# Loading the first chunk's q and k in rows of 1 KB by halves of the heads, and masking the third tile on VectorE

## The chip, the core and the metric

The kernel runs on one core of a Trainium2 chip. The metric is device time in microseconds (us); lower is better. Before the change it is 223.19 us, the median of 3 runs (222.91 to 223.42). TensorE multiplies matrices, VectorE (DVE) and ScalarE (ACT) work on tiles, GpSimd (POOL) does small work and issues DMAs, and SyncE (SP) issues DMAs; ACT can issue them too.

## What is computed

Windowed attention with sinks over 4 batches, 8 heads, 768 tokens and a head size of 64, then a normalised MLP with a residual. Inputs and output are float32.

```python
scores = scale * np.matmul(q, k.transpose(0, 1, 3, 2))
keep = is_sink | in_window          # 4 sinks, window of 128 tokens, causal
scores = np.where(keep, scores, -1000000000.0)
a = softmax(scores)
x = matmul(a, v), heads side by side  # [4, 768, 512]
xn = (x - mu) / np.sqrt(var + 1e-06) * g_ln
out = x + np.maximum(xn @ w_ch1, 0.0) @ w_ch2   # w_ch1 512 x 2048, w_ch2 2048 x 512
```

## The kernel before

The 3072 tokens are 24 tiles of 128; two tiles are a chunk, three chunks a batch. For each tile the kernel gets q and k with the head dimension on the partitions (`kT`, `qT`: four head pairs of 128 rows), computes transposed scores against its own and the preceding tile's keys (L681, L726), takes the exponential on ScalarE (`ex`, L685 and L740) and multiplies by v (`av`, L763 and L768). VectorE divides by the row sum (`rec` L781, `x` L783), takes the statistics (`st` L787, L789) and subtracts the mean (`xc` L791). `xc` is transposed (L804), scaled into `xnt` (L815), and goes through the MLP: `ph` (L830 by tile for the first two chunks, L837 by chunk after), relu (`h`, L847 on ScalarE, L849 on VectorE), `pc` (L866), the residual (L874) and the store (L878).

Nothing is issued in program order. Every operation is entered with `P.op` as a record of the engines that may run it, their times, a priority, and its dependences. `Plan.run` then walks a model of the engines and DMA queues, and what it finds is written out as each engine's fixed order. Constants such as `HW_F` (the model of the first loads: time a DMA keeps the queue, its start, its end) change nothing on the chip but the order. An engine runs its list strictly in that order and waits at the first instruction that is not ready. A ring is a set of buffers taken in turn; `pair` is two slots of two PSUM banks each, for scores and values, `one` single banks.

The first chunk (tiles 0 and 1 of batch 0) is loaded apart from the others. `chunk(0)` issues four DMAs of 256 KB in float32, k on SP and q on ACT (L563): for each tile, partitions 0 to 63 hold k and 64 to 127 hold q, two neighbouring tokens to a partition, which makes rows of 2 x 64 x 4 = 512 B in `natf`. ScalarE and VectorE each cast four heads to bf16 (`natc`, L570); eight matmuls with the identity turn the tile (L580), and their outputs are interleaved in PSUM, so that the two tokens of a partition come to stand next to each other; ScalarE and VectorE evict them into `kT` and `qT` (L547). Tiles 2 and 3 come by GpSimd's DMAs with a cast (`nat`, L596), are transposed (L601) and evicted (also L547).

The masks of the first tiles are made in one of two ways. For a tile number below `PAR["pm"]`, TensorE first adds `neg`, a matrix of large negative numbers, to the scores' banks (`pm`, L668, two matmuls of 512 columns for a bank pair), and exp makes zeros of them. From `PAR["pm"]` on, VectorE multiplies the exponentials with `mask` (`mk`, L688, 128 x 1024 in bf16). `pm` is 3 before the change: tiles 0, 1 and 2 by TensorE.

Also in VectorE's list is `vs` (L506): the sinks' v spread over the heads, from `vc`, which eight small DMAs on SP's queue bring (L502), issued after natf and `gt` (L498). TensorE's list begins with some matmuls on zeros (L932) that keep it busy until data comes.

Of the kernel before, what the change touches and what calls it, by code (L numbers as in the profile page):

```python
# [7 lines left out]
FP32 = mybir.dt.float32  # L8
BF16 = mybir.dt.bfloat16
# [188 lines left out]
def pe(us):  # L198
    return {"PE": (us, us + Plan.PE_DRAIN)}


def act(n):
    t = 0.065 + 0.000833 * n
    return (t, t + 0.105)


def dve(n, per=1.04):
    t = 0.067 + 0.001 * per * n
    return (t, t + 0.09)


def fix(occ, extra=0.09):
# [2 lines left out]

SW = (0.9, 0.7, 0.9)
SW_W = (2.65, 0.7, 0.9)
HW_F = (0.8, 2.2, 0.5)
HW_S = (0.75, 0.8, 1.2)
HW_X = (1.0, -0.2, 0.6)  # L220
SW_2 = (0.65, 0.7, 0.9)
# [4 lines left out]
NEVER = -1e9  # L226

PAR = dict(strict=40.0, win=0.4, tr=-8.0, sc=-5.0, sc1=-2.0, av=2.0, trx=9.0, by_dma=4, x_by_dma=3,
           w1p=(1.6, 2.6, 2.7, 2.8), pm=3, w2p=(4.5, 4.51, 4.52, 4.53), by_tile=2, vp=(0.0, 0.1, 2.0, 2.1, 4.2, 4.3), ld1=0.05)


def general(tc, nc, slots, pairs, ones, ident_f, ident, w1, w2, mhalf, g_s, g_r, q, k, v, out, scale):


    V, A, G, T, DMA = nc.vector, nc.scalar, nc.gpsimd, nc.tensor, nc.gpsimd.dma_start
    B, H, S, D = q.shape
# [4 lines left out]
    v_n = [flat(f32["qT"][2]), flat(f32["kT"][3])]  # L241
    qT, kT, ksT = f32["kT"][0], f32["kT"][1:3], f32["kts"][0]
    ks_n, vs_n = flat(f32["pe"][6]), flat(f32["pe"][7])
    sc = [t.rearrange("p a b c -> p (a b c)").rearrange("p (h c) -> p h c", h=4) for t in slots["natf"]]
    aT = [[flat(f32["pe"][2 * i + a]) for a in range(2)] for i in range(3)]
    xs, os_, xn, xnt, h1 = slots["ot"][0:2], slots["ot"][2:4], slots["xc"][0], slots["xnt"][0], slots["h1"]
    mx, sm = g_r[:, 0, :], g_r[:, 1, :]
# [6 lines left out]
    with tc.For_i(0, B, 1) as b:  # L254
# [5 lines left out]
        for r in range(RB):  # L260
            x, cur, prev = xs[r % 2], r % 2, (r + 1) % 2
# [8 lines left out]
            for a in range(HP):  # L270
                s_ps = pairs[a % 2]
                for h2 in range(2):
# [4 lines left out]
                    if r > 1:  # L277
                        T.matmul(s_ps[:, h2, 256:256 + NS], lhsT=qT[rows, a, :], rhs=ksT[rows, a, 0:NS],
                                 start=True, stop=True)
# [33 lines left out]
            for a in range(2):  # L313
                for i, rows in ((0, 128), (1, 128), (2, NS)):
                    for h in range(4):
                        src = g_s[:, 4 * a + h, :] if i == 2 else sc[a][:, h, 128 * i:128 * i + 128]
# [18 lines left out]
            pb = ones[0].bitcast(BF16)  # L335
# [5 lines left out]
            for u in range(8):  # L341
                for s in range(2):
                    ht = 2 * u + s
                    for j in range(4):
                        T.matmul(ones[u % 2][:, 256 * s:256 * s + 256], rhs=xnt[:, j, :], start=j == 0, stop=j == 3,
                                 lhsT=w1[ht // 4][:, j, 128 * (ht % 4):128 * (ht % 4) + 128])
                A.activation(h1[u], ones[u % 2], AF.Relu)
            for i in range(2):
                for ht in range(16):
                    at = 256 * (ht % 2) + 128 * i  # L350
                    T.matmul(ones[2 + i], lhsT=h1[ht // 2][:, at:at + 128], rhs=w2[ht // 4][:, ht % 4, :],
                             start=ht == 0, stop=ht == 15)
# [6 lines left out]
def kernel(  # L359
# [12 lines left out]
    nc = tc.nc  # L372

    B, H, S, D = q.shape
# [17 lines left out]
    P = Plan()  # L392

    def ring(name, n, shape, dtype, pool=consts):
        P.ring(name, [Slot(pool.tile(shape, dtype, name=f"{name}{i}"), f"{name}{i}") for i in range(n)])
# [3 lines left out]
    ones = [psum.tile([128, 512], FP32, name=f"one{i}") for i in range(4)]  # L399
    P.ring("pair", [Slot(pairs[i], f"pair{i}", banks[2 * i:2 * i + 2]) for i in range(2)])  # L400
    P.ring("one", [Slot(ones[i], f"one{i}", [banks[4 + i]]) for i in range(4)])
    ring("natf", 2, [128, H, 2, 64], FP32)
    ring("natc", 2, [128, 2, H, 64], BF16)
    ring("nat", 8, [128, H, 64], BF16)
    ring("vn", 7, [128, H, 65], BF16)
    ring("kT", 4, [128, HP, 256], BF16)
# [14 lines left out]
    ident_f, ident = const("ident_f", [128, 128], FP32), const("ident", [128, 128], BF16)  # L421
# [17 lines left out]
    Bc = {n: Buf(n) for n in names}  # L439
# [7 lines left out]
    V, G = nc.vector, nc.gpsimd  # L447
# [35 lines left out]
    def negs(e):  # L483
# [15 lines left out]
         writes=[Bc["gt"]], dma=HW_T)  # L499
    for h in range(H):  # L500
# [3 lines left out]
            reads=[Bc["vc"]], writes=[Bc["vcd"]], dma=HW_T)  # L504
    for b in range(B):
# [3 lines left out]
            reads=[Bc["vcd"], Bc["vc"], Bc["sel"]], writes=[Bvs[b]], nb=12.0 if b == 0 else 40.0 * b)  # L509
# [6 lines left out]
    for c in range(4):  # L516
        P.op(f"w2ld{c}", {"POOL": (0.75, 0.8)}, PAR["w2p"][c], lambda e, c=c: G.dma_start(
            w2[c], moe_w_ch2[512 * c:512 * (c + 1), :].rearrange("(t p) n -> p t n", p=128)),
            writes=[Bw2[c]], dma=SW_W)
# [5 lines left out]
    x_b, xst_b, kT_b, qT_b, vn_b, kts_b = {}, {}, {}, {}, {}, {}  # L525
# [3 lines left out]
    tile_of, scores, trs = {}, {}, {}  # L529
# [15 lines left out]
    def evict(name, prio, n, src, dst, reads, writes, fp=False):  # L545
        du = {"ACT": act(n), "DVE": dve(n) if fp else dve(n, 0.52)}
        P.op(name, du, prio, lambda e: (nc.scalar.copy if e == "ACT" else V.tensor_copy)(dst(), src()),  # L547
             reads=reads, writes=writes)

    def chunk(c):  # L550
        b, R = c // RC, c % RC
        d = at(c, "tr") if c >= 2 else early(2 * c)
        ld = d - 14.0 if c >= RC else 4.0
        if c < 2:
            kT_b[c], qT_b[c] = Buf(f"kT{c}", "kT"), Buf(f"qT{c}", "qT")
            for t in (2 * c, 2 * c + 1):
                d, at_t = early(t), slice(128 * (t % 2), 128 * (t % 2) + 128)
                if c == 0:
                    nat, src, parts = Buf(f"n{t}", "natc"), Buf(f"f{t}", "natf"), [Buf(f"{nm}l{t}") for nm in "kq"]
                    for i, x in enumerate((k, q)):  # L560
                        ap = x[b, :, 128 * t:128 * t + 128, :].rearrange("h (p i) d -> p h (i d)", i=2)
                        P.op(f"{'kq'[i]}ld{t}", {("SP" if i == 0 else "ACT"): (0.53, 0.53)}, -70 + t,
                             lambda e, src=src, ap=ap, i=i: (nc.sync if e == "SP" else nc.scalar).dma_start(  # L563
                                 src.t[64 * i:64 * i + 64].rearrange("p h i d -> p h (i d)"), ap),
                             writes=[src, parts[i]], dma=HW_F)
                    cut = [Buf(f"c{t}{hh}") for hh in range(2)]
                    for hh in range(2):
                        hs = slice(4 * hh, 4 * hh + 4)
                        P.op(f"cast{t}{hh}", {"DVE": dve(512), "ACT": act(512)}, d + 0.01 * hh,
                             lambda e, nat=nat, src=src, hs=hs: (nc.scalar.copy if e == "ACT" else V.tensor_copy)(  # L570
                                 nat.t[:, :, hs], src.t[:, hs].rearrange("p h i d -> p i h d")),
                             reads=parts, hold=[src], writes=[nat, cut[hh]])

                        pt = Buf(f"pt{t}{hh}", "one")

                        def tr(e, nat=nat, pt=pt, hh=hh):
                            pb = pt.t.rearrange("p (n h m i) -> p n h m i", n=2, h=2, i=2)
                            for hp in range(2):
                                for i in range(2):
                                    nc.tensor.matmul(pb[:, :, hp, :, i], lhsT=nat.t[:, i, 4 * hh + 2 * hp:4 * hh + 2 * hp + 2, :],  # L580
                                                     rhs=ident, start=hp + i == 0, stop=True, skip_group_check=True)
                        trs[t] = [P.op(f"tr{t}{hh}", pe(0.3), d + 0.02 + 0.01 * hh, tr,
                                       reads=[cut[hh], Bc["ident"]], hold=[nat, kT_b[c], qT_b[c]], writes=[pt])]
                        for i, T in enumerate((kT_b[c], qT_b[c])):
                            tile_of["kq"[i], t, hh] = Buf(f"{'kq'[i]}T{t}{hh}")
                            evict(f"ev{'kq'[i]}{t}{hh}", d + 0.05 + 0.01 * i, 256,
                                  lambda pt=pt, i=i: pt.t[:, 256 * i:256 * i + 256].rearrange("p (h c) -> p h c", h=2),
                                  lambda T=T, at_t=at_t, hh=hh: T.t[:, 2 * hh:2 * hh + 2, at_t], [pt],
                                  [T, tile_of["kq"[i], t, hh]], fp=True)
                else:  # L590
                    pt = Buf(f"pt{t}", "one")
                    for i, (x, T) in enumerate(((k, kT_b[c]), (q, qT_b[c]))):
                        nat = Buf(f"{'kq'[i]}n{t}", "nat")
                        ap = x[b, :, 128 * t:128 * t + 128, :].rearrange("h p d -> p h d")
                        P.op(f"{'kq'[i]}ld{t}", {"POOL": (0.87, 0.9)}, PAR["ld1"] + 0.2 * (t - 2) + 0.01 * i,
                             lambda e, nat=nat, ap=ap: G.dma_start(nat.t, ap), writes=[nat], dma=SW)  # L596

                        def tr(e, nat=nat, pt=pt, i=i):
                            pb = pt.t.bitcast(BF16)
                            for hp in range(HP):  # L600
                                nc.tensor.transpose(pb[:, 512 * i + 128 * hp:512 * i + 128 * hp + 128],  # L601
                                                    nat.t[:, 2 * hp:2 * hp + 2, :], ident)
                        trs[t] = [P.op(f"tr{t}{i}", pe(0.3), d + 0.02 + 0.01 * i, tr,
                                       reads=[nat, Bc["ident"]], hold=[T], **({"rw": [pt]} if i else {"writes": [pt]}))]
                        done = Buf(f"{'kq'[i]}T{t}")
                        for hh in range(2):
                            tile_of["kq"[i], t, hh] = done
                        evict(f"ev{'kq'[i]}{t}", d + 0.05 + 0.01 * i, 512,
                              lambda pt=pt, i=i: pt.t.bitcast(BF16)[:, 512 * i:512 * i + 512].rearrange("p (h c) -> p h c", h=HP),
                              lambda T=T, at_t=at_t: T.t[:, :, at_t], [pt], [T, done])  # L610
        else:
            for nm, src, bT in (("k", k, kT_b), ("q", q, qT_b)):
                T = Buf(f"{nm}T{c}", nm + "T")
                bT[c] = T
                pt = Buf(f"pt{nm}{c}", "one")
                for i in range(2):
                    if c >= PAR["by_dma"]:
                        nat = Buf(f"{nm}n{c}{i}", "nat")
# [294 lines left out]
    t = 1.2  # L913
# [62 lines left out]
```

## Time and profile before

| what | value |
|---|---|
| median of 3 runs | 223.19 us |
| the profiled execution | 223.16 us |
| its span | 221.7 us |
| TensorE busy | 212.5 us, 96% |
| VectorE, ScalarE, GpSimd busy | 117.4, 110.3, 89.7 us |
| the chain that ended last, TensorE's part | 89% |
| the chain, DMA of `natf` | 3.0% |
| first L830 run of 48 matmuls starts on the chain | 24.30 us |

The profile is of one execution. A line such as `L570 ACT CAST natc<-natf` names the source line, the engine, the operation, what is written and what is read. "Idle before" is the engine's waiting, and the name behind it is what ended it. The chain is followed back from the last instruction: at each step to what released it, or to the instruction before it on its engine. "issue" is time in which the engine waited for nothing that the profile shows. TensorE is busy for nearly the whole span, so only the first 24 us, in which it waits for others, hold time that is not matmuls.

### The profile page before, as it was taken

What the parts mean: (1) busy time and instruction counts of PE and PEld (TensorE: products, weight loads), DVE (VectorE), ACT (ScalarE), POOL (GpSimd) and SP (SyncE); (2) the same over time, 40 slices, a digit from 0 to 9 for tenths busy, and PEclk for the clock granted to TensorE, in tenths of its full rate; (3) what the DMA queues carried; (4) which work ended last, traced back from release to release, by engine and by line L of the source; (5) the groups of instructions that cost most, each with busy time, mean ns of one, the idle gap of its engine ahead of it and who ended that gap; (6) DMA issues with size and microseconds to landing.
All of it is one profiled execution on the core that took longest, in us unless ns stands there. A gap on an engine that the chain in (4) does not pass through costs nothing.

```text
span 221.7 us, 5208 instructions
## 1 busy us (share of the span) xinstructions
PE 212.5 (96%) x2100; PEld 146.0 (66%) x2100; DVE 117.4 (53%) x264; ACT 110.3 (50%) x169; POOL 89.7 (40%) x130
## 2 busy tenths in 40 slices
PE   6788999999999999999999999999999999999992
PEld 2456997674864874874864964964964964965861
DVE  5679833494797744744724824735715715732011
ACT  2567656346446456455447447445446447441600
POOL 7888693669173533652352641650110110120000
PEclk9999999999999999999999999999999999999998
DMA  5999999999999899999899999999533321121102
GB/s 129 166 179 205 177 190 206 165 186 156 181 180 156 127 119 136 142 132 117 139 118 125 115 144 120 139 126 117 124 46 93 101 46 47 50 47 50 47 37 74
DMA packets 108575, 27.45 MB, mean 124 GB/s; under 512 B 99200, under 2 KB 105600, under 8 KB 108544
## 3 DMA queue, kind: packets, MB, share of 16 engines
q0 software_dynamic: 74944, 13.11, 83.6%
q1 hardware_dynamic: 32400, 13.28, 28.5%
q10 hardware_dynamic: 1200, 0.66, 1.3%
q8 instruction: 18, 0.29, 0.6%
q14 instruction: 13, 0.11, 0.2%
HBM read 27.30 MB, written 6.29 MB: 152 GB/s over the span
## 4 chain that ended last, share of the span: by engine, by line
PE 89%; DVE 4%; DMA 3%; issue 1%; SPq 0%; ACT 0%; DVEq 0%; ACTq 0%
PE one L866 38%; PE one L837 32%; PE one L830 5%; PE pair L726 5%; PE pair L768 4%; DMA natf<-in_k_dram 3%; PE pair L763 2%; DVE st L787 1%; PE one L635 1%; PE one L730 1%; DVE x L783 1%; DVE xnt L815 1%; PE one L804 1%; PE one L580 0%; PE pair L668 0%
## 5 line engine op out<-in xcount | busy, mean ns | idle before, releaser
L866 PE MATMUL one<-w,h 128*128 128x512 bf16 (+1 forms) x400 | 89.0, 371 | 0.0
L847 ACT ACTIVATE h<-one 128x512 bf16<-128x512 f32 x94 | 56.1, 597 | 58.8 <-PE one L837 43.5
L837 PE MATMUL one<-xnt,w 128*128 128x256 bf16 x640 | 74.4, 273 | 0.0
L837 PEld LDWEIGHTS <-w 128*128 128x128 bf16 x640 | 61.4, 98 | 9.0
L866 PEld LDWEIGHTS <-h 128*128 128x128 bf16 x400 | 37.2, 98 | 38.5 <-issue 2.1
L744 DVE TENSOR_TENSOR pe<-pe,mask 128x1024 bf16<-128x1024 bf16 (+1 forms) x40 | 25.9, 649 | 56.7 <-ACT pe L740 55.9
L740 ACT ACTIVATE pe<-pair 128x1024 bf16<-128x1024 f32 (+1 forms) x40 | 36.2, 957 | 32.1 <-PE pair L726 32.1
L621 POOL DMA_DIRECT2D nat<-in_k_dram x16 | 14.3, 893 | 38.8 <-DMA kT<-nat 25.3
L874 DVE SCALAR_TENSOR_TENSOR ot<-one,st,x 128x512 f32<-128x512 f32 (+1 forms) x25 | 18.1, 725 | 19.4 <-PE one L866 19.3
L796 POOL TENSOR_SCALAR st<-st 128x1 f32<-128x1 f32 x24 | 7.3, 303 | 45.1 <-DVE st L789 44.1
L541 POOL DMA_DIRECT2D vn<-in_v_dram x24 | 22.0, 918 | 4.3 <-DMA w<-in_moe_w_ch_dram 3.0
L621 POOL DMA_DIRECT2D nat<-in_q_dram x16 | 14.5, 907 | 14.7 <-DMA qT<-nat 12.0
L787 DVE BATCH_NORM_STATS2 st<-x 128x6 f32<-128x512 bf16 x24 | 16.6, 694 | 0.8
L783 DVE TENSOR_TENSOR x<-pair,rec 128x512 bf16<-128x512 f32 x24 | 16.6, 691 | 0.8
L830 PE MATMUL one<-xnt,w 128*128 128x128 bf16 x256 | 16.0, 219 | 0.0
L797 POOL TENSOR_TENSOR st<-st,mhalf 128x1 f32<-128x1 f32 x24 | 14.7, 613 | 2.0
L830 PEld LDWEIGHTS <-w 128*128 128x128 bf16 x256 | 14.6, 98 | 0.7
L768 PE MATMUL pair<-vn,pe 128*128 128x65 bf16 x352 | 14.6, 193 | 0.5 <-ACT pe L685 0.5
L768 PEld LDWEIGHTS <-pe 128*128 128x128 bf16 x352 | 13.9, 97 | 1.3 <-issue 0.5
L726 PEld LDWEIGHTS <-kT 64*128 64x128 bf16 x216 | 6.9, 94 | 8.4 <-issue 8.1
L726 PE MATMUL pair<-qT,kT 64*128 64x128 bf16 (+1 forms) x216 | 11.6, 238 | 0.0
L781 DVE RECIPROCAL rec<-pair 128x8 f32<-128x8 f32 x24 | 4.8, 199 | 12.1 <-PE pair L768 12.0
(83 smaller groups left out, 120.5 us busy)
## 6 DMA issues: line engine op xcount, KB each, us to landing
out_dram<-ot SPq DMA_DIRECT2D x23, 256.0 KB
w<-in_moe_w_ch_dram POOLq DMA_DIRECT2D x8, 512.0 KB, 10.2
vn<-in_v_dram POOLq DMA_DIRECT2D x24, 128.0 KB, 6.4
nat<-in_k_dram POOLq DMA_DIRECT2D x22, 128.0 KB, 5.9
nat<-in_q_dram POOLq DMA_DIRECT2D x22, 128.0 KB, 5.5
natf<-in_k_dram SPq DMA_DIRECT2D x2, 256.0 KB
natf<-in_q_dram ACTq DMA_DIRECT2D x2, 256.0 KB
xnt<-xc SPq DMA_TRANSPOSE x18
```

The source lines that it names most:

```text
L541: P.op(f"vld{t}", {"POOL": (0.87, 0.9)}, prio, lambda e: G.dma_start(bv.t[:, :, 0:64], v[b, :, 128 * r:128 * (r + 1), :].rearrange("h p d ...
L621: lambda e, nat=nat, ap=ap: G.dma_start(nat.t, ap), writes=[nat], dma=SW)
L726: nc.tensor.matmul(pp.t[:, h2, col:col + q1 - q0], lhsT=kt.t[rs, hp, k0:k0 + 128], rhs=qT.t[rs, hp, q0:q1], start=i == 0, stop=True, skip_ ...
L740: P.op(f"ex{c}{hp}", {"ACT": act(2 * n)}, d + 0.1 + 0.05 * j, lambda e, pp=pp, pb=pb: nc.scalar.activation(pb.t[:, :, 0:n], pp.t[:, :, 0:n ...
L744: V.tensor_mul(pb.t[:, :, 0:n], pb.t[:, :, 0:n], mm),
L768: nc.tensor.matmul(po.t[:, h // 4, 65 * (h % 4):65 * (h % 4) + 65], lhsT=part(h, n), rhs=vn_b[tv].t[:, h, :], start=(not R and h % 4 == 0 ...
L783: P.op(f"x{t}", {"DVE": dve(512)}, d + 0.11, lambda e: V.tensor_tensor(x.t.rearrange("p (a h c) -> p a h c", a=2, c=64), pv()[:, :, :, 0:6 ...
L787: P.op(f"bn{t}", {"DVE": fix(0.60)}, d + 0.12, lambda e: V.bn_stats(st.t[:, 8:14], x.t), reads=[x], writes=[st, mv])
L830: nc.tensor.matmul(ph.t[:, 128 * s:128 * s + 128], lhsT=w1[u // 2][:, j, 128 * s:128 * s + 128], rhs=xnt.t[:, j, 128 * (u % 2):128 * (u % ...
L837: nc.tensor.matmul(ph.t[:, 256 * s:256 * s + 256], lhsT=w1[ht // 4][:, j, 128 * (ht % 4):128 * (ht % 4 + 1)], rhs=xnt.t[:, j, :], start=j ...
L847: nc.scalar.activation(hb.t, ph.t, AF.Relu)
L866: nc.tensor.matmul(pc.t[:, 0:wd], lhsT=(h1[2 * s + i].t[:, 128 * ii:128 * ii + 128] if by_tile else h1[ht // 2].t[:, 256 * (ht % 2) + 128 ...
```

## The change

The four loads of the first chunk are cut by halves of the heads instead of by tiles: each brings 256 tokens of four heads, four neighbouring tokens to a partition, in rows of 4 x 64 x 4 = 1 KB. So `natf` and `natc` become one buffer of twice the size. A cast and a group of four transposing matmuls now belong to a head pair, not to a tile and half; the outputs are interleaved by four in PSUM, and one eviction writes a head pair of both tiles. `PAR["pm"]` becomes 2, so tile 2 is masked by VectorE. `HW_F` is changed as well. As the planner's input differs, the order of the engines' lists differs too in the first part. On GpSimd and SP the order is the same. Up to the L830 run of 48 matmuls:

- TensorE: all 16 matmuls L580 first, then tile 0's and half of tile 1's scores, tile 0's values before the transposes of tile 2; tile 3's values and one more L830 group move ahead of the third `xc` transposes (L804); the four `neg` matmuls of tile 2 and two on zeros in the middle are gone, and one of the ten on zeros at the start.
- VectorE: the two evictions of tile 2 and one relu go to ScalarE; `vs` moves from behind the second `xc` to behind the first; the four masks of tiles 2 and 3 stand before the third `rec`.
- ScalarE: four evictions of k follow the two casts, then the exponentials of tile 0 and of half of tile 1.

The core of the diff:

```diff
-HW_F = (0.8, 2.2, 0.5)
+HW_F = (0.65, 1.9, 0.6)
...
-           ... pm=3, ...
+           ... pm=2, ...
...
-    ring("natf", 2, [128, H, 2, 64], FP32)
-    ring("natc", 2, [128, 2, H, 64], BF16)
+    ring("natf", 1, [128, H, 4, 64], FP32)
+    ring("natc", 1, [128, 4, H, 64], BF16)
...
-            for t in (2 * c, 2 * c + 1):
-                    for i, x in enumerate((k, q)):
-                        ap = x[b, :, 128 * t:128 * t + 128, :].rearrange("h (p i) d -> p h (i d)", i=2)
...
-                            for hp in range(2):
-                                for i in range(2):
-                                    nc.tensor.matmul(pb[:, :, hp, :, i], lhsT=nat.t[:, i, 4 * hh + 2 * hp:4 * hh + 2 * hp + 2, :],
-                                                     rhs=ident, start=hp + i == 0, stop=True, skip_group_check=True)
...
+            if c == 0:
+                nat, src = Buf("n0", "natc"), Buf("f0", "natf")
+                for hh in range(2):
+                    hs, parts = slice(4 * hh, 4 * hh + 4), [Buf(f"{nm}l{hh}") for nm in "kq"]
+                    for i, x in enumerate((k, q)):
+                        ap = x[b, hs, 0:256, :].rearrange("h (p i) d -> p h (i d)", i=4)
...
+                    for hp in (2 * hh, 2 * hh + 1):
+                        cut, pt, two = Buf(f"c{hp}"), Buf(f"pt0{hp}", "one"), slice(2 * hp, 2 * hp + 2)
+                        P.op(f"cast{hp}", {"DVE": dve(512), "ACT": act(512)}, d + 0.01 * hp,
+                             lambda e, two=two: (nc.scalar.copy if e == "ACT" else V.tensor_copy)(
+                                 nat.t[:, :, two], src.t[:, two].rearrange("p h i d -> p i h d")),
+                             reads=parts, hold=[src], writes=[nat, cut])
...
+                            pb = pt.t.rearrange("p (n m i) -> p n m i", n=2, i=4)
+                            for i in range(4):
+                                nc.tensor.matmul(pb[:, :, :, i], lhsT=nat.t[:, i, two, :], rhs=ident, start=i == 0,
+                                                 stop=True, skip_group_check=True)
...
+                            evict(f"ev{'kq'[i]}0{hp}", d + 0.05 + 0.01 * hp, 256,
+                                  lambda pt=pt, i=i: pt.t[:, 256 * i:256 * i + 256], lambda T=T, hp=hp: T.t[:, hp, :], [pt],
+                                  [T, tile_of["kq"[i], 0, hh], tile_of["kq"[i], 1, hh]], fp=True)
```

## The prediction

> **What bounds the kernel now.** I read the chain that ended last first, in order of time, to 25 us (start, length, what).
>
> ```profile
> 1.83 6.56 DMA natf<-in_k_dram
> 8.47 0.63 ACT natc L570
> 9.15 1.05 PE one L580 x8
> ...
> 13.03 0.22 DVE rec L781
> ...
> 20.19 0.66 DVE h L849
> ...
> 22.79 0.36 DVE xc L791
> ...
> 23.20 0.40 PE one L804 x4
> 23.59 0.22 PE pair L763 x2
> 23.82 0.48 PE pair L768 x16
> ```
>
> From 24.30 us on the chain is TensorE nearly without a break to 217.6 us, and the change adds nothing to it. So the question is when L830 can begin its 48 matmuls, 24.30 us now. Before that stand a transfer (to 8.4), casts, transposes and evictions of tile 1 (to 11), then VectorE without a gap from 13.03 to 23.15.
>
> Next the DMA by stretches (the last two columns are the share of 16 DMA engines and GB/s), then one of a late store in rows of 2 KB.
>
> ```profile
> 2.50:3.30 0.80, 0.80 (x3) 0.30 (x2) 0.72 (x3) 0.80 (x1) 0.80 (x2) 1.00 0.56 145
> 3.30:4.30 1.00, 1.00 (x4) 0.32 (x3) 0.83 (x7) 0.64 (x2) 1.00 (x2) 1.00 1.13 311
> 4.30:6.70 2.40, 1.29 (x6) 0.41 (x5) 0.71 (x1) 0.62 (x1) 2.40 (x4) 1.00 1.22 227
> ```
> ```profile
> DMA packets 93, 0.19 MB, mean 381 GB/s; under 512 B 0, under 2 KB 0, under 8 KB 93
> ```
>
> The first three stretches hold natf alone, in rows of 512 B: 227, 623 and 1096 packets. All but 48 are rows, so 150 of 2048 are left at 6.70, and at 457 per us they end at 7.03. The casts start at 8.47, 1.44 later. Counted from 2.5 us the rows run at 472 per us up to 4.3 and 463 up to 6.7: a slow start, a second of catching up at 311 GB/s, then a steady supply. I read that as a limit per row, since the engines moved 311 GB/s of the same rows when a backlog stood.
>
> Last the timeline where the first softmax runs.
>
> ```profile
> 9.00 1.02 ACT L685 ACTIVATE pe<-pair 128x1024 bf16<-128x1024 f32 x1
> ...
> 11.43 1.94 ACT L685 ACTIVATE pe<-pair 128x1024 bf16<-128x1024 f32 x2 [0.81 <-PE pair L681]
> ...
> 12.50 0.42 PE L768 MATMUL pair<-vn,pe 128*128 128x65 bf16 x8 [0.34 <-ACT pe L685]
> ```
>
> Tile 0's exp starts 0.44 us after its last eviction (8.56), but its values (L768) come at 12.50, behind tile 1's scores; `rec` at 13.03 follows by 0.53.
>
> **The transfer.** 2048 rows of 512 B become 1024 of 1 KB; bytes, the number of DMAs (two on SP, two on ACT) and their issue order stay. If rows are the limit, the slow start (227 rows in 0.8 us) moves 232 KB instead of 116. The other 816 KB take 2.62 us at 311 GB/s, ending at 2.5 + 0.8 + 2.62 = 5.92; with the same 1.44 us the second pair of casts starts at 7.36, 1.11 earlier. Bounds: at 381 GB/s 2.14 us, casts at 6.88; at today's pace 8.47. I take 311, the rate shown by this very transfer; 381 is a store of rows twice as long. The first half's casts come earlier still and wait in no one's way, but VectorE and ScalarE then stand at the second half's casts.
>
> One rule speaks against this. The Trainium skill, "SBUF — State Buffer", section "Door 1: The DMA port swizzle (why `[64,N]` ≈ `[32,N]`)", says that a transfer into partitions 0 to 63, or 64 to 127, reaches half of the ports, 218 GB/s at most, and that rows do not matter to that. The 227 GB/s above look like it; the full microsecond at 311 does not. By the rule the 1.05 MB end no sooner than 7.3 us and the sum below would be a loss of about 0.6 us.
>
> **Casts to the first exp.** In both kernels ScalarE and VectorE cast 512 values a lane each (0.62 and 0.74 us). Tile 0 used to need only the first loads; now it needs all four. After 7.36: cast to 7.98; ScalarE evicts k of head pairs 0 and 1 (L547, two in 0.81) to 8.79, then pairs 2 and 3 to 9.60; VectorE's q of pair 3, which waits for ScalarE's eviction of the same bank as today (0.97 us at 7.70), runs 9.63 to 10.05. That is 2.69 us after the casts, against 2.51 today (8.47 to 10.98). The transposes of pairs 2 and 3 lie beside it: eight of L580 in 1.05 us with 0.31 for the last are 0.105 apiece, so 0.42 a pair. Their outputs now stand 16 bytes apart instead of 8; no row shows that. Bounds: 0.057 us (L601's pace, contiguous), no gain as ScalarE's order sets the end; double, 0.210, which makes the last eviction 0.74 late. I take 0.105: neighbours are apart in both.
>
> With 0.44 us as above tile 0's exp starts at 10.49, takes 0.97 (two in 1.94), the values start 0.10 later at 11.56, and `rec` at 12.09: 0.94 earlier than 13.03. The evictions of tile 2 (0.42 and 0.41 at 12.20 and 12.54), which stood before `rec`, go to ScalarE.
>
> **VectorE from `rec` to the third `xc`.** Today 13.03 to 23.15, 10.12 us. Out goes one relu (L849, 0.66 to the next start, 0.68 taken; ScalarE has it now). In come two masks of the third tile, and the fourth tile's second mask, which moves ahead of the third `rec`: 3 x 0.60 (the chain's pace of L688; the group's mean is 0.65). 10.12 - 0.68 + 1.80 = 11.24, so `xc` ends at 23.33. ScalarE must feed it: from 10.49 seven exps of 0.97, four copies of 0.50 (0.48 to 0.58 at 16.0), two small exps of 0.25 and about 0.7 of waits for scores end the last exp at 20.5; VectorE reaches that mask about 8.3 after `rec`, at 20.4, and loses 0.15. `xc` ends at 23.48.
>
> **After it.** Today 0.05, then the transposes L804 and tile 3's values (0.40, 0.22, 0.48) precede L830. Now tile 3's values stand ahead of `xc` in TensorE's order, so 0.05 and 0.27 (L804's pace at 26.98) remain: L830 x48 at 23.80, 0.50 earlier than 24.30. The four removed matmuls with `neg` (0.22 each, from four in 0.86) save nothing themselves: TensorE waits for VectorE there. Without that cover they would be worth 0.86. The next `xc` comes at 26.5, just as the 48 matmuls end (23.80 + 2.68 = 26.48), so nothing is to spare. The third quarter's weights are no wait: GpSimd saw w's second piece landed at 21.43, and TensorE wants it near 22.0. GpSimd's own list of DMAs is unchanged.
>
> **One wait moves.** `vs` of batch 0 (L506) waits for eight small loads of `vc`. It stands at 18.26 today and moves ahead of tile 0's `xnt`, to `rec` + 2.25 = 14.34. SP's queue moves the last rows thus:
>
> ```profile
> q1 hardware_dynamic: 20, 0.00, 6.1%
> ```
>
> That is 13.6 to 14.2 us; with 1.44 they land near 15.6, harmless today. The last `vc` is issued at 9.35, behind natf and gt; if all that moves with natf by 1.11 it lands at 14.5, a wait of 0.16, which the 0.15 above absorbs. If nothing moves, the wait is 1.26. Behind it stand `xnt`, the second `rec` and `x`, and through `x` the bank for tile 2's scores and its exp. I take the first: these loads follow natf in the same queue.
>
> **Sum.** Profiled execution 223.16 us (span 221.70, 1.46 around it), which the median, 223.19, matches: 223.16 - 0.50 = 222.66, so **222.65 us**, own range 222.2 to 223.0, chance 0.48.
>
> **Rivals.** (1) Bytes, not rows, limit the half-tile loads: 227 GB/s holds for 2.4 us, more than twice the catch-up. Casts stay at 8.47 and everything comes 1.11 later: 223.8; half of the gain gives 223.2. Slower from casts later than 7.86. Chance 0.24. (2) `vs` stalls VectorE by about 1.1 beyond what is absorbed: 223.75; for it, the last rows come in bursts 1.2 to 1.6 us apart between GpSimd's transfers (around 11.0, 12.5 and 13.9), which need not move with natf; against it, they are issued behind it. Slower from a wait of 0.65. Chance 0.16, the doubled transpose counted in. (3) Rows run at 381 GB/s: 0.48 better, 222.2. Chance 0.12.
>
> What this measurement can tell from no change is about 0.2%, 0.45 us. Faster by more: 0.36 of the first case (its sum is just past the line, its range leans to it) and all of the last, 0.48. Slower: 0.16 of (1) and 0.12 of (2), 0.28. Within: 0.24. The range 222.0 to 223.8 holds all but the tails of the rivals.
>
> **What would show it.** Right: natf's rows over by 6 us, second casts near 7.4, tile 0's exp near 10.5, first `rec` near 12.1, `vs` without idle before it, L830 x48 near 23.8. Wrong: second casts after 7.9, L580's eight over 1.2 us, idle time before `vs` or before the mask L688, or TensorE waiting after 24 us.

## The result, and the profile after

The changed kernel takes 226.01 us, the median of 4 runs (225.28 to 226.82), against 223.31 (222.91 to 223.55) of the kernel before in the same session: a ratio of 1.0124, 95% interval 1.0085 to 1.0163. It is slower by 2.7 us, where 222.65 and a gain were forecast. The mean granted clock of its four executions is 0.986 to 0.992, against 0.996 to 1.000 in the executions of the kernel before that ran beside the experiments. The profiled execution took 225.28, with a span of 223.8.

The chain of waits of the changed kernel, up to 26 us (start, length, what):

```profile
1.83 6.47 DMA natf<-in_k_dram
...
8.38 0.63 ACT natc L572
9.00 0.05 issue
9.05 1.66 PE one L579 x8
10.71 0.85 PE pair L667 x2
11.57 0.54 PE pair L680 x7
...
13.77 0.22 DVE rec L780
...
16.06 0.70 DVE vs L506
...
21.19 1.80 DVE pe L687 x3
...
24.82 0.36 DVE xc L790
25.18 0.05 issue
25.23 0.40 PE one L803 x4
25.63 0.39 PE one L829 x7
```

(Lines below the diff have numbers one smaller than before: L579 is the old L580, L829 the old L830.) The casts of the second loads start at 8.38, where 7.36 was forecast and 8.47 was measured before: the transfer has gained only 0.09 us. Then the eight transposes take 1.66 us, not 1.05, and L829's 48 matmuls begin at 25.63, not at 23.80. From the transposes on the chain goes through tile 0's scores and values and then VectorE's list.

The DMA of the changed kernel by stretches (columns as in the prediction; the last is GB/s):

```profile
2.50:3.30 0.80, 0.80 (x3) 0.30 (x2) 0.72 (x3) 0.80 (x1) 0.80 (x2) 1.00 0.55 132
3.30:4.30 1.00, 1.00 (x4) 0.32 (x3) 0.83 (x7) 0.61 (x2) 1.00 (x2) 1.00 0.95 299
4.30:6.70 2.40, 1.51 (x5) 0.33 (x4) 0.69 (x1) 0.62 (x1) 2.40 (x4) 1.00 1.13 237
```

The shape is that of before, 145, 311 and 227 GB/s, with half as many rows. So the rows were not the limit. From 6.2 to 6.6 us only SP's queue still moves rows, which is k into partitions 0 to 63, at 243 GB/s; from 4.3 to 5.5 us, with k and q moving at once into both halves, it was 238. The two halves did not add up.

TensorE of the changed kernel by stretches (stretch, its length, PE's busy time and matmuls, granted clock, DMA share, GB/s):

```profile
8.50:9.25 0.75, 0.20 (x3) 1.00 2.37 154
9.25:9.50 0.25, 0.25 (x4) 0.65 2.44 156
9.50:12.50 3.00, 3.00 (x18) 0.50 2.35 158
12.50:12.75 0.25, 0.25 (x2) 0.52 1.58 183
12.75:24.00 11.25, 9.09 (x172) 1.00 1.43 198
```

For 3.4 us, from 9.33 to 12.73, TensorE ran at half its clock. Before the change the clock on record is 1.00 until the last matmul. What is new ahead of it is idle time between the two groups of transposes. After:

```profile
6.67 1.05 PE L579 MATMUL one<-ident,natc 128*128 128x128 bf16 x8 [0.89 <-ACT natc L572]
9.05 1.66 PE L579 MATMUL one<-ident,natc 128*128 128x128 bf16 x8 [1.34 <-ACT natc L572]
```

and before:

```profile
6.65 1.05 PE L580 MATMUL one<-ident,natc 128*128 128x128 bf16 x8 [1.11 <-ACT natc L570]
9.15 1.05 PE L580 MATMUL one<-ident,natc 128*128 128x128 bf16 x8 [0.24 <-ACT natc L570]
```

Now TensorE waits 0.89 us for the first transposes and 1.34 us for the second ones, as nothing of tile 0 can run between the halves: its scores need the heads of both. Before, it waited 1.11 and 0.24 us, with `neg` and scores of tile 0 in between.

Last, the timeline of the end. After:

```profile
218.98 0.48 DVE L873 SCALAR_TENSOR_TENSOR ot<-one,st,x 128x256 f32<-128x256 f32 x1 [0.73 <-PE one L865]
```

and before:

```profile
217.71 0.48 DVE L874 SCALAR_TENSOR_TENSOR ot<-one,st,x 128x256 f32<-128x256 f32 x1 [0.73 <-PE one L866]
```

The last `ot` begins 1.27 us later, but the span is 2.1 longer: from there to the end it is 223.8 - 218.98 = 4.82 us, against 221.7 - 217.71 = 3.99. Part of the loss lies behind the last computation.

### The profile page after: what moved, and what is told of

It reads as the page before. It is cut to its first block, busy times and chain, and to the rows that moved or that the text cites. A ratio compares the mean times of both kernels' runs of the same rounds, so it can differ in the third digit from the quotient of the medians.

```text
span 223.8 us, 5173 instructions
## 1 busy us (share of the span) xinstructions
PE 211.0 (94%) x2073; PEld 145.8 (65%) x2093; DVE 117.2 (52%) x263; ACT 110.9 (50%) x169; POOL 90.0 (40%) x130
## 4 chain that ended last, share of the span: by engine, by line
PE 88%; DVE 5%; DMA 3%; issue 1%; SPq 0%; ACT 0%; DVEq 0%; ACTq 0%
PE one L865 37%; PE one L836 31%; PE one L829 5%; PE pair L725 5%; PE pair L767 4%; DMA natf<-in_k_dram 3%; PE pair L762 1%; DVE pe L687 1%; DVE st L786 1%; DVE x L782 1%; PE one L634 1%; PE pair L667 1%; PE one L579 1%; PE one L729 1%; DVE xc L790 1%
## 5 line engine op out<-in xcount | busy, mean ns | idle before, releaser
L865 PE MATMUL one<-w,h 128*128 128x512 bf16 (+1 forms) x380 | 86.8, 370 | 1.6 <-issue 0.9
L846 ACT ACTIVATE h<-one 128x512 bf16<-128x512 f32 x95 | 56.7, 597 | 59.9 <-PE one L836 44.6
L795 POOL TENSOR_SCALAR st<-st 128x1 f32<-128x1 f32 x24 | 7.9, 327 | 48.5 <-DVE st L788 47.4
L829 PE MATMUL one<-xnt,w 128*128 128x128 bf16 x256 | 16.0, 219 | 0.0
L829 PEld LDWEIGHTS <-w 128*128 128x128 bf16 x256 | 14.6, 98 | 0.5
```

Source lines behind the costliest of these rows:

```text
L829: nc.tensor.matmul(ph.t[:, 128 * s:128 * s + 128], lhsT=w1[u // 2][:, j, 128 * s:128 * s + 128], rhs=xnt.t[:, j, 128 * (u % 2):128 * (u % ...
L846: nc.scalar.activation(hb.t, ph.t, AF.Relu)
L865: nc.tensor.matmul(pc.t[:, 0:wd], lhsT=(h1[2 * s + i].t[:, 128 * ii:128 * ii + 128] if by_tile else h1[ht // 2].t[:, 256 * (ht % 2) + 128 ...
```

## The experiments

The experiments are edits of the changed kernel, alone or together, except the two that say "the kernel before". C is the theory that the low clock costs the time, P that writing 64 partitions at a time limits the transfer, M that the masks on VectorE cost it, L that the other order of the lists does; the rivals are in the expectations. The kernel before was run beside each.

**Six matmuls on zeros between the two groups of transposes** of the changed kernel, behind the operation `tr01`:

```diff
+    at = next(o.start for o in order if o.name == "tr01")
+    items.append((at + 1e-4, -6, pairs[1][:, 0, :]))
     items.sort(key=lambda z: (z[0], z[1]))
```

> The changed kernel with six matmuls on zeros (512 columns) between the transposes of the first and of the second half, where TensorE stood idle from 7.7 to 9.05 us. Theory C (the idle time cost TensorE its clock, 0.50 from 9.4 to 12.6 us, and that half rate lies on the path): clock 1.00 throughout, the second eight of L579 in 1.05 us instead of 1.66, tile 0's exp near 11.1 instead of 12.15, L829 x48 near 24.6 instead of 25.63, time near 225.0 (about 1.0 below the changed kernel). Rival L (the half rate is hidden; the loss is the order, since tile 0 now waits for both halves): clock 1.00 but L829 x48 stays near 25.6 and the time near 226.

Measured: 227.6 (six runs: 224.52 and 224.6, and four from 227.52 to 227.82), ratio 1.0139 [1.0083, 1.0195]. Two values 3 us apart from one program. In the profiled execution, one of the long ones, the first transposes already went at the slow pace and the six matmuls behind them took 0.43 us each, so they held up the second transposes until 10.71; a later stretch then had the low clock on record:

```profile
20.75:24.00 3.25, 3.17 (x33) 0.50 1.23 204
```

So the filler was too long where the clock was already low, and the first gap was still open. Inconclusive for the price. But the program is the changed kernel's up to the first transposes, which took 1.05 us there and 1.89 here: the pace differs between executions.

**The kernel before with `pm` = 2 alone:** `pm=3` becomes `pm=2`.

> The kernel before with pm = 2 alone: the third tile's masks by VectorE, the loads as they were. Theory C: the loads and the clock are the loss, so this costs little: VectorE gets two masks of 0.60 us in its gapless stretch and TensorE loses 0.86 us of work that it did while waiting, between -0.1 and +0.8 us. Rival M (the mask on VectorE is the main loss): +1.5 us or more.

Measured: 223.68, ratio 1.0017 [1.0000, 1.0033]. By the ratio the masks cost some 0.4 us there, at the edge of what can be told from nothing. The profile does not show where: its last `ot` starts 0.36 us later (218.07), but its second casts already start 0.32 later (8.79), with the same loads. M as the main loss falls.

**The loads over all 128 partitions,** two tokens to a partition, so in rows of 512 B again, but by halves of the heads as in the change:

```diff
-  ap = x[b, hs, 0:256, :].rearrange("h (p i) d -> p h (i d)", i=4)
+  ap = x[b, hs, 0:256, :].rearrange("h (p i) d -> p h (i d)", i=2)
-  src.t[64 * i:64 * i + 64, hs].rearrange(...)
+  src.t[:, hs, 2 * i:2 * i + 2].rearrange(...)
-  pb = pt.t.rearrange("p (n m i) -> p n m i", n=2, i=4)
-  nc.tensor.matmul(pb[:, :, :, i], ...
+  pb = pt.t.rearrange("p (n m i) -> p n m i", n=2, i=2)
+  nc.tensor.matmul(pb[:, i // 2, :, i % 2], ...
```

> The changed kernel with each of the four loads spread over all 128 partitions, two tokens to a partition, rows of 512 B again: same bytes, same number of DMAs, twice the rows. Theory P (a load into 64 partitions is limited in bytes, about 230 GB/s, whatever the rows): natf runs above 300 GB/s, its rows end near 6.0 us, the second casts start near 7.4 instead of 8.38, TensorE's gap shrinks below 1 us and its clock stays, L829 x48 near 24 and the time 222.5 to 224. Rival R (rows are the limit): no faster than the loads before, casts at 8.4 or later, time 226.

Measured: 223.19, ratio 0.9994 [0.9979, 1.0009], 2.8 us less than the changed kernel. Its DMA by stretches:

```profile
2.50:3.30 0.80, 0.80 (x3) 0.30 (x2) 0.72 (x3) 0.80 (x1) 0.80 (x2) 1.00 0.59 134
3.30:4.30 1.00, 1.00 (x4) 0.32 (x3) 0.83 (x7) 0.34 (x2) 1.00 (x2) 1.00 1.15 344
...
4.30:5.50 1.20, 1.20 (x4) 0.29 (x2) 0.38 (x1) 0.38 (x1) 1.20 (x2) 1.00 1.18 309
```

its timeline:

```profile
7.08 0.62 ACT L572 CAST natc<-natf 128x512 bf16<-128x512 f32 x1 [1.34 <-DMA natf<-in_q_dram]
...
7.75 1.05 PE L579 MATMUL one<-ident,natc 128*128 128x128 bf16 x8 [0.71 <-ACT natc L572]
...
11.61 0.21 DVE L780 RECIPROCAL rec<-pair 128x8 f32<-128x8 f32 x1 [1.56 <-PE pair L767]
```

and its chain of waits:

```profile
22.45 0.36 DVE xc L790
...
23.25 2.68 PE one L829 x48
```

309 GB/s holds where the changed kernel has 237, with rows half as long. The second casts come at 7.08 and `rec` at 11.61, both earlier than the forecast's 7.36 and 12.09, and L829's 48 matmuls start at 23.25, 1.05 ahead of the kernel before. The gap before the second transposes shrinks to 0.71 us, and the clock on record is 1.00 throughout the head. The edit leaves the engines' lists and the masks as they are in the changed kernel, so this pair compares best: from the second casts to tile 0's exp it is 2.91 us (7.08 to 9.99) where the changed kernel takes 3.77.

**The six matmuls on zeros with `pm` = 3.**

> The first experiment with pm = 3, so the third tile is masked by TensorE as before. Theory C with my sum: VectorE's stretch loses two masks, 1.2 us, but ScalarE's last exp then sets its end, so 0.2 to 0.6 us below the first experiment. Rival M: 1.5 us or more below it.

Measured: 224.05, ratio 1.0055 [1.0029, 1.0081]. Again there are two groups: seven runs from 223.56 to 224.27, five from 225.3 to 225.72. The profile is of the lower one: the six took 1.50 us, at the full pace, and the second transposes 1.05. As two groups stand in both kernels with six, the difference of the medians does not price the masks.

**Fillers for both gaps:** two more matmuls on zeros at the start, and three in the second gap.

```diff
+    items.append((1.202, -2, pairs[1][:, 0, :]))
+    items.append((at + 1e-4, -3, pairs[1][:, 0, :]))
```

> The changed kernel with both of TensorE's gaps filled: two more matmuls on zeros at the start (0.43 us each, idle before 6.67 us goes from 0.89 to 0.05) and three between the two groups of transposes (0.75 to 1.3 us in a gap of 1.34). Theory C (the low clock from 9.35 to 12.6 us is what the new gaps cost): the granted clock is 1.00 throughout, the second eight L579 take 1.05 instead of 1.66, tile 0's exp starts at 11.3 instead of 12.15, rec at 12.9 instead of 13.77, and the time is 225.0 (224.5 to 225.4) with no second group of runs 3 us higher. Rival (the order and the masks cost it, TensorE has slack here): the clock is 1.00 and the time stays 226.0. Rival (the gaps are not what sets the clock): a stretch at 0.50 stays somewhere before 25 us.

Measured: 224.44, ratio 1.0052 [1.0039, 1.0066]. Six of the seven runs lie between 224.28 and 224.54; the profiled one is the seventh, 226.31, with the second transposes at the full pace (1.05) but a low clock later, behind a stretch in which TensorE waited three times, 0.42 to 0.59 us, between short groups of matmuls:

```profile
19.75:23.25 3.50, 3.50 (x38) 0.52 1.24 205
```

The median is a little below the 224.5 to 225.4 expected and 1.57 us under the changed kernel's, with nothing altered but matmuls on zeros. The profiled run is 226.31 - 224.44 = 1.87 above the median, but not all of that is the low clock's: its second casts start at 8.91, half a microsecond later than in the other profiles of these loads (8.38 to 8.43). The gaps are shorter in it, 0.44 and 0.96 us, and not closed.

**Fillers for both gaps and `pm` = 3.**

> The same with pm = 3, so the third tile's masks are TensorE's again. Theory M (two masks of 0.6 us each and the mask moved ahead cost VectorE about 1 us before the third xc): 0.8 to 1.0 less than the kernel with only the gaps filled, 224.1. Rival (masks are hidden, TensorE or ScalarE sets the third xc): within 0.3 of it, 225.0. Together with the clock's part the rest to the kernel before, 0.8 or less, is the second casts at 8.4 with tile 0 behind them, and the end.

Measured: 223.87, ratio 1.0030 [1.0017, 1.0044]; 0.57 less, between theory M's 0.8 and its rival's 0.3. All eight runs lie between 223.57 and 224.4. The clock on record is 1.00 up to the last matmul, and the head in the timeline is:

```profile
9.11 1.05 PE L579 MATMUL one<-ident,natc 128*128 128x128 bf16 x8 [0.72 <-ACT natc L572]
...
11.34 1.94 ACT L684 ACTIVATE pe<-pair 128x1024 bf16<-128x1024 f32 x2 [0.78 <-PE pair L680]
```

With the casts at 8.43, tile 0's exp starts 2.91 us after them; 3.77 in the changed kernel. TensorE still waits 0.92 us before the first transposes: the eleven matmuls on zeros took the 4.02 us of the changed kernel's nine, so TensorE had its full pace earlier.

**All partitions, gap filled** with two matmuls on zeros.

> The loads over 128 partitions in rows of 512 B, with two matmuls on zeros between the groups of transposes, where TensorE was idle for 0.71 us. Theory C: its clock was 1.00 in the profile without them, so nothing is gained in most runs: 223.2, with the upper runs (224.3) gone. Rival (the gap costs something in every run): 222.7.

Measured: 223.28, ratio 0.9997 [0.9986, 1.0009]. Nothing gained, as expected where the clock was not low. Without the filler one run of twelve took 224.34, with the lowest mean clock of them, 0.986; here none is above 223.44.

**All partitions, `pm` = 3.**

> The loads over 128 partitions in rows of 512 B, with pm = 3. If transfer and masks are separate terms (P and M), the 0.8 to 1.0 us of the masks comes off 223.2: 222.3, faster than the kernel before. Rival (with the transfer 1.3 us earlier VectorE has time for the masks, or TensorE's four matmuls with neg and the planner's other order cost as much): 223.2 or more.

Measured: 222.61 (222.46 to 223.17), ratio 0.9975 [0.9961, 0.9989]: faster than the kernel before, by little. But the last `ot` starts at 216.77, and at 216.61 with `pm` = 2: taking the masks away gave nothing up to there (216.38 in the repetition below, 0.23 earlier). Most of the gain is from the last `ot` to the end, 4.2 us against 4.9.

**The end.** Since 4.8 to 5.0 us stood there in every profile of the new loads with `pm` = 2, and 4.2 to 4.5 with `pm` = 3, ScalarE got four more small exps (with `pm` = 2; the edit shown) or two more (with `pm` = 3) in its first idle time:

```diff
-  lambda e: nc.scalar.activation(one_e[:, 1:2], one_e[:, 0:1], AF.Exp)
+  lambda e: [nc.scalar.activation(one_e[:, 1:2], one_e[:, 0:1], AF.Exp) for _ in range(5)]
```

> The loads over 128 partitions in rows of 512 B, pm = 2, with four more one-column exps on ScalarE while it waits for the first data (0.2 us each, before 5.1 us). From the start of the last ot to the end of the span it was 4.9 us in every kernel of the new loads with pm = 2, 4.2 to 4.5 with pm = 3 and 4.0 before; the last packets there are of instructions. Theory E (where ScalarE's code for the end lies decides what is fetched last; pm = 3 has two ScalarE instructions fewer): the end moves, to 4.0 to 4.4, and the time to 222.5. Rival (another engine's code, or what the masks do earlier): the end stays 4.9 and the time 223.2.

> The loads over 128 partitions with pm = 3 and two more such exps on ScalarE, which gives it as many instructions as with pm = 2. Theory E: the end goes from 4.2 to 4.9 us and the time from 222.6 to 223.2, which would mean that pm = 3 gained by the end alone. Rival: 4.2 and 222.6 stay.

Measured: 223.05, ratio 0.9989 [0.9978, 1.0000], end 4.9; and 222.84, ratio 0.9975 [0.9962, 0.9989], end 4.5. Theory E falls by the first, where the end should have become 4.0 to 4.4. In the second it is 4.5, within what `pm` = 3 showed before and not the 4.9 that E asked for. The second run repeats that all partitions with `pm` = 3 beat the kernel before.

**The kernel before with a slow start of TensorE:** five matmuls on zeros at the start instead of ten.

```diff
         n = int((o.start - t - 0.45) / (0.43 if t < 8 else 0.25))
+        n = min(n, 5) if t < 2 else n
```

> The kernel before with five instead of ten matmuls on zeros at the start: TensorE is idle from 3.9 to 6.65 us (1.1 us idle before). Nothing else is changed. Theory C (an idle TensorE in the head gets a low clock for some 3.3 us, and that is paid at the end): the first eight L580 take 1.7 to 1.9 us instead of 1.05, the scores of tile 0 follow late, and the time is 223.8 to 224.8. Rival (TensorE has slack until the second casts at 8.4, so a slow start is hidden): 223.2.

Measured: 224.40 (223.76 to 225.22), ratio 1.0049 [1.0031, 1.0068]: 1.1 us slower with loads, order and masks as before. Its timeline, and then TensorE's stretch from 6.5 us on:

```profile
6.84 1.89 PE L580 MATMUL one<-ident,natc 128*128 128x128 bf16 x8 [2.77 <-ACT natc L570]
8.44 1.14 PE L668 MATMUL pair<-neg,ident 128*128 128x512 bf16 x2
...
10.05 1.89 PE L580 MATMUL one<-ident,natc 128*128 128x128 bf16 x8
```
```profile
6.50:13.00 6.50, 6.16 (x30) 1.00 2.19 160
```

Both groups of transposes run at the slow pace, though the clock on record is 1.00. The transposes' own duration, 1.05 or 1.89, tells more than the record. The rival, that a slow start is hidden, falls.

## Why the prediction was wrong

Its sum can be laid beside the profiled execution, step by step:

| step | forecast | measured | off |
|---|---|---|---|
| second casts start | 7.36 | 8.38 | +1.02 |
| from there to tile 0's exp | 3.13 | 3.77 | +0.64 |
| exp to `rec` | 1.60 | 1.62 | +0.02 |
| `rec` to the end of the third `xc` | 11.39 | 11.41 | +0.02 |
| from there to L829 x48 | 0.32 | 0.45 | +0.13 |
| L829 x48 to the last `ot` (unchanged) | 193.41 | 193.35 | -0.06 |
| last `ot` to the end of the span (unchanged) | 3.99 | 4.82 | +0.83 |
| around the span | 1.46 | 1.48 | +0.02 |

222.66 and the 2.62 us of the last column make 225.28, the time of that execution.

**The step that failed first is "I read that as a limit per row".** Half the rows moved the same bytes at the same rates, and spreading each DMA over 128 partitions raised the steady rate from 237 to 309 GB/s with rows of 512 B. The rival of bytes was right, and its 223.8 is what the transfer's miss alone makes of the sum (222.66 + 1.02 = 223.68). The full microsecond at 311 GB/s, which decided against it, did not last: 299 and then 237 came again with half the rows. The Trainium skill, "SBUF — State Buffer", section "Door 1: The DMA port swizzle (why `[64,N]` ≈ `[32,N]`)", which the prediction weighed and set aside, had the steady rate nearly right: 218 GB/s at most for 64 partitions, 227 to 243 here, so somewhat more than it allows. It gives that limit by ports alone; that rows do not matter to it was the prediction's reading, and the runs bear it out. By its own working of that rule (rows over at 7.3 us, casts 1.44 later) the prediction would have had a loss of about 0.9 and not 0.6.

**The second is a term that was not in the sum: TensorE's clock.** The prediction took 0.105 us for each transpose and kept it; at the full pace that is right (1.05 for eight, also at the new spacing in PSUM). Of TensorE's waiting it says that the removed `neg` matmuls "save nothing themselves: TensorE waits for VectorE there", and it put no price on new waits. But with the new gap came the low clock, and the transposes and `neg` matmuls in it stand on the chain: 0.64 us above the forecast in the profiled execution. In all eight profiles of the new loads whose second transposes ran at the full pace and unhindered, that step takes 2.91 us. So the forecast's 3.13 was itself 0.22 too long, and the low clock cost 0.86. The fillers took 1.57 off the median. The other three executions of the changed kernel were up to 1.5 us longer than the profiled one; that a low clock falls on a worse place in them, as at 19.75 in the kernel with the fillers, is likely and not shown.

**The third is the end,** 0.83 us, taken as unchanged. The last packets there are of instructions, and their number does not tell (7 after, 7 in the best kernel, 6 before). The longer end goes with the new loads at `pm` = 2 (4.8 to 5.0 us; 4.1 in the kernel before with `pm` = 2), and four more instructions on ScalarE did not shorten it; its cause stays open.

**Against the kernel before** the profiled executions differ by 2.12 us. From the second casts to the last `ot` it was 209.24 us, and is 210.60 in the changed kernel and 209.53 with all partitions, the same lists and the same masks. So by single executions 0.29 us of the loss goes with the other order (L) and the masks together, and 0.83 with the end. The remaining 1.07 are not there with all partitions, and 0.86 of them lie ahead of tile 0's exp, in the stretch of the low clock. The casts are 0.09 earlier.

**Right were** VectorE's term, 11.39 against 11.41, with `vs` running directly behind `xc` (so that rival fell), and exp to `rec`. The masks' 0.6 a piece were right within that term; that taking them away gained nothing up to the last `ot` with the loads over 128 partitions means that something else sets the time there, another wait or the order that comes with `pm` = 3; no run tells which.

The steps from the changed kernel to the best one, taken in this order, are 1.57 for the fillers, 0.57 for `pm` = 3, and 1.26 for all partitions (from 223.87 to 222.61, without fillers). In another order they divide otherwise: all partitions alone took off 2.82, the low clock with it. The forecast gain of the head is real with that layout: with it L829's 48 matmuls began 0.55 earlier than the 23.80 forecast, and yet 223.19 came out, since the end took 0.9 us back (216.61 to 221.5, where 3.99 stood before).

## What to carry to other kernels

Read the limit of a transfer from its longest steady stretch, and test it with a layout that changes one thing: rows or partitions. When a change moves idle time on TensorE, the idle time can have a price of its own, in the pace of the matmuls after it; compare durations of one shape (here eight transposes, 1.05 or 1.66 to 1.89 us) before calling a wait hidden. Compare the stretch after the last computation too before explaining a span. And before a difference late in a trace is put down to an edit, compare where the first loads landed: with the same loads the second casts started up to half a microsecond apart.

## What was not expected of the hardware

- A low clock lasts 3.4 us at 0.50 (9.33 to 12.73, 20.70 to 24.11, 19.87 to 23.29) and came in some executions of a program and not in others. The Trainium skill, "TensorE: Matmul & The Clock Gate", section "Part 1: The HAM clock gate (the "warmup" mystery)", gives a free-running window of about 3.4 us and half rate after an idle one, which agrees with the length and with the scatter. But no window ahead of it was idle here: in the 3.41 us before the three stretches TensorE was busy for 1.32, 2.09 and 1.96 us, and in the last two no wait was longer than 0.6 us. How much idle time it takes no run here shows.
- The clock on record can read 1.00 while eight transposes take 1.89 us instead of 1.05 (6.5 to 13.0 us in the last experiment).
- The end of the span, from the start of the last `ot`, is 4.0 to 5.0 us long, by program, with the same stores to come.
